# Second layer's begin: narrow products for the second group's queries and the first group's wo, fewer idle products behind w2

## The chip, the core and the metric

The kernel runs on one core of one Trainium2 chip. A core has TensorE (PE: matrix products; its loads of weights are listed as PEld), VectorE (DVE), ScalarE (ACT), GpSimd (POOL) and SyncE (SP), which here issues nearly all DMA transfers from HBM. The engines run side by side, each through its own instructions in order, and wait for one another by semaphores. SBUF holds the operands, PSUM takes the products. The metric is the device time of the core in microseconds (us); less is better.

## The reference

A decoder with two layers at one position: attention with 32 heads over a cache of 4,096 keys and values, then an MLP with a hidden width of 1,376, and the same again with the same weights and the same cache. All numbers are float32.

```
def _A_ref(x, k_cache, v_cache, wq, wo):
    q = (x @ wq) in 32 heads of 128
    scores = q . k_cache * 128 ** -0.5
    p = softmax(scores)
    o = p . v_cache
    return o @ wo                           # (1, 1, 512)

def _B_ref(x, w1, b1, w2, b2):
    h = gelu(x @ w1 + b1)                   # 1376 wide
    return h @ w2 + b2

x = A_x                                     # (1, 1, 512)
x = x + _A_ref(_layernorm(x), ...)
x = x + _B_ref(_layernorm(x), ...)
x = x + _A_ref(_layernorm(x), ...)
x = x + _B_ref(_layernorm(x), ...)
```

Keys and values are 67 MB each, and each layer needs them all; the kernel moves 285.9 MB.

## The kernel before, in words

**Groups.** The 32 heads are done in eight groups of four. A group's keys, like its values, are 8,192 KB: eight blocks of 128 partitions x 2,048 floats (`NC`), four quarters of 512 (`U`) each. A group is: queries (x by the group's 1,024 KB of wq), scores (64 PE records into `pS`), softmax weights (`exponentials`: maximum on DVE, exponential on ScalarE; `weights`: PE transposes into `pO`, which is also `pT`), values (64 records into `pO`, or for most groups three blocks on PE and five on DVE), `head` (which brings four heads' results into columns), and the product with the group's wo.

**Narrow and wide.** A product with one row of x or of the heads can be put to PE in two ways. The wide form (`wide_query_block`, L338, and the `else` of `out_product`, L281) takes a 128-column stationary operand from `x_wide` or `on_wide` and 512 moving columns: four products, eight PE records, since each is two passes; the answer is turned by four DVE transposes of 32x128 (`turned(..., wide=True)`, L148). The narrow form (`query_block`, L191, and the `if last` branch, L278) has one or two stationary columns and 128 moving ones, four products to each quarter, 32 records; its answer is turned by a single transpose of 128x128 (L150). Before, the second layer's first group has narrow queries (`first_queries`, L451), its second group wide ones (`next_queries`, L464). wo is narrow only at the end of each layer, and there it goes to `pS`.

**The arena.** Nearly all of SBUF is one tile, `arena`, with three homes for blocks of keys or values (`A_AT`, `B_AT`, `C_AT`), an area `SHARED` for w1, w2 and later a group's wq, and an area `PAIR` for a pair of weights (one group's wo and another's wq). `SCRATCH` overlaps the end of `SHARED`'s w2.

**The second layer's begin.** The first layer ends with group 7. Its keys (in `C_AT`) and values (in `A_AT`) stay, and so do group 6's values (in `B_AT`, six quarters of them parked in PSUM, `pK`, and copied back by ScalarE at L473). The second layer therefore takes group 7 first, with no load, then group 6, whose keys are loaded again into whatever comes free, then group 5 and so on. I call them the second layer's first, second and third group. The loads stand in SP's queue in this order:

1. w2's five pieces into `SHARED`, behind w1's products;
2. the second group's wq in two halves, into the place of w2's blocks 0 to 3, behind w2's blocks 1 and 3 (`behind_w2`, L435); 1,024 KB and 512 KB of its keys behind blocks 7 and 9;
3. 1,024 KB of its keys into `PAIR + NC`, behind the first group's queries (L454); then 1,024, 1,024 and 3,328 KB into `C_AT`, behind the first group's scores of block 0, 1 and 5 (L458, L460);
4. a pair of weights into `C_AT + 24 U`, behind the first group's scores (L462);
5. the third group's keys, 8,192 KB into `A_AT`, behind the first group's values (L487);
6. the third group's values: 6,144 KB into `C_AT`, behind the second group's scores, and 2,048 KB over the pair of weights, behind the third group's queries (L489, pieces (0, 6) and (6, 8));
7. the next pair, the fourth group's keys, and so on.

SP takes these one by one, and a load that has to wait holds up all behind it. PE takes its products in the order of the program (`keep_in_program_order`, L84); the order on DVE and ScalarE is the tile framework's.

**The idle products.** `idle` (L165) multiplies zeros; its result is never read. In `mlp`, where `load_w2` is given (the first layer's MLP), one of 512 columns stands behind w2's blocks 4, 7 and 9, and one of 256 behind block 10, the last.

Of the kernel before, what the change touches and what calls it, by code (L numbers as in the profile page):

```python
# [17 lines left out]
P = 128  # L18
# [7 lines left out]
FB = 11  # L26
W1C = FJ * J
EPS = 1e-5
U = 512
# [24 lines left out]
def decode_layers(ctx: ExitStack, tc: tile.TileContext, x, k, v, w, w1, b1, w2, b2, out):  # L54
# [10 lines left out]
    def small(name, n=1):  # L65
        if name not in places:
            a = sum(b - a for a, b in places.values())
            places[name] = a, a + n
        a, b = places[name]
        assert b <= 120 and b - a == n  # L70
        return smalls[:, a:b]
# [3 lines left out]
    def at(first, n):  # L75
        return arena[:, first : first + n]

    def load(first, src):
        t = at(first, src.shape[-1])
        tc.keep_in_program_order(nc.sync.dma_start(t, src))  # L80
        return t

    def matmul(*a, **kw):
        tc.keep_in_program_order(nc.tensor.matmul(*a, **kw))  # L84
# [7 lines left out]
    def of_w(row, i, n):  # L92
        return w[row][:, NC * i : NC * (i + n)]

    def by_four(t):
        return t.rearrange("p (j n) -> p j n", j=4)


    wq_t = by_four(load(SHARED, of_w(1, 0, 1)))
# [18 lines left out]
    pS, pO = (psum.tile([P, 512], F32, name=n) for n in ("pS", "pO"))  # L118
# [9 lines left out]
    def of_32(t, n, i=0):  # L128
        return t[:, : 32 * n].rearrange("p (c q) -> p c q", q=32)[:, :, i]
# [6 lines left out]
    def in_quarters(t, n):  # L136
        return t[:, : 32 * J].rearrange("p (j n) -> p j n", j=J)[:, :, :n]

    def pairs(t):
        return t[:, :8].rearrange("p (c i) -> p c i", i=2)  # L140

    def turned(src, wide=False):

        t = work.tile([P, P], F32, name="turned")
        if wide:
            for j in range(J):
                q = slice(32 * j, 32 * j + 32)
                nc.vector.transpose(t[q], src[q, P * j : P * (j + 1)])  # L148
        else:
            nc.vector.transpose(t, src[:, :P])  # L150
        return t
# [13 lines left out]
    def idle(to, n=U):  # L165
        matmul(to[:, :n], zero[:, 0:1].to_broadcast([P, P]), at(C_AT, n), start=True, stop=True)
# [22 lines left out]
    def query_block(c, xs, wt):  # L189
        for j in range(J):  # L190
            matmul(pO[32 * j : 32 * j + 2, :P], pairs(xs)[:, c, :], wt[:, c, P * j : P * (j + 1)],  # L191
                   start=(c == 0), stop=(c == 3))

    def queries(to, negm, wide=False):
        qt = turned(to, wide)
        z = zq
        nc.vector.scalar_tensor_tensor(z[:, :, C - 1], of_32(qt, J, 1), negm, of_32(qt, J),
                                       op0=ALU.mult, op1=ALU.add)
        return z
# [55 lines left out]
    def head(rl, last=False):  # L255
        ot = at(SCRATCH, U)
        nc.vector.transpose(ot, pO)  # L257
        o, on = small("o", 4), on_wide
        own = at(SCRATCH, 4 * 129).rearrange("p (b q) -> p b q", q=129)[:, :, :P]
        own = own.rearrange("p b (d q) -> p d b q", q=32)[:, :, :, 0]  # L260
        nc.vector.tensor_reduce(o, own, axis=AX.X, op=ALU.add)
        if last:
            nc.vector.tensor_scalar(on[:, :4], o, rl, None, op0=ALU.mult)
        else:
            nc.vector.tensor_scalar(in_quarters(on, 4), o.unsqueeze(1).to_broadcast([P, J, 4]), rl, None,  # L265
                                    op0=ALU.mult)
        return on

    def head_out(rl, wt, last=False):
        on = head(rl, last)  # L270
        out_product(on, wt, last)
        return of_32(turned(pS) if last else turned(pO, wide=True), 4)

    def out_product(on, wt, last=False):
        for d in range(4):
            if last:
                for j in range(J):
                    matmul(pS[32 * j : 32 * j + 1, :P], on[:, d : d + 1], wt[:, d, P * j : P * (j + 1)],  # L278
                           start=(d == 0), stop=(d == 3))
            else:  # L280
                matmul(pO, on[:, d : d + P], wt[:, d, :], start=(d == 0), stop=(d == 3))  # L281

    def mlp(xs, s, w1_t, w2_t, load_w2=None, behind_w2=None):
        xb = small("xb", 4)
        nc.gpsimd.tensor_tensor(xb, pairs(xs)[:, :, 0], b2c, op=ALU.add)
        for c in range(4):
            for j in range(J):
                matmul(pO[32 * j : 32 * j + 2, :FJ], pairs(xs)[:, c, :], w1_t[c][:, FJ * j : FJ * (j + 1)],
                       start=(c == 0), stop=(c == 3))
            if c == 0:  # L290
                nm, ss = mean_of(xs, s)
            if c == 1:
                r = rstd_of(ss)
            if load_w2:
                load_w2(c)
        idle(pS)
        ht = at(SCRATCH, 32 * FB)
        nc.vector.transpose(ht, pO[:, : 32 * FB])
        h, u, a, z, t, g = (small(f"gelu_{i}", FB) for i in "huaztg")
        nc.vector.scalar_tensor_tensor(h, of_32(ht, FB, 1), nm, of_32(ht, FB), op0=ALU.mult, op1=ALU.add)  # L300
        if load_w2:
            load_w2(4)
        nc.vector.scalar_tensor_tensor(u, h, r, b1c, op0=ALU.mult, op1=ALU.add)
        nc.vector.scalar_tensor_tensor(a, u, 0.044715, u, op0=ALU.mult, op1=ALU.mult)
        nc.vector.scalar_tensor_tensor(z, a, 1.0, u, op0=ALU.add, op1=ALU.mult)
        nc.scalar.activation(t, z, AF.Tanh, scale=float(np.sqrt(2.0 / np.pi)))
        nc.vector.scalar_tensor_tensor(g, t, 1.0, u, op0=ALU.add, op1=ALU.mult)
        for c in range(FB):
            for j in range(J):
                matmul(pS[32 * j : 32 * j + 1, :P], g[:, c : c + 1], w2_t[c][:, P * j : P * (j + 1)],  # L310
                       start=(c == 0), stop=(c == FB - 1))
            if load_w2:
                behind_w2(c)
                if c in (4, 7, 9):
                    idle(pO)
                elif c == FB - 1:
                    idle(pO, U // 2)
        return of_32(turned(pS), 4), xb

    def load_w1(first, a, b):  # L320
# [14 lines left out]
    xs, s = set_x(zero, 1.0, xcol)  # L335
# [19 lines left out]
    def next_queries(xs, negm, wt, to=pO):  # L355
        for c in range(4):
            wide_query_block(to, c, xs, wt)
        z = queries(to, negm, wide=True)
        if to is pS:
            nc.vector.memset(pS, 0.0)  # L360
        return z

    def add_up(acc, own):
        t = small("acc", 4)
        nc.vector.scalar_tensor_tensor(t, own, 1.0, acc, op0=ALU.mult, op1=ALU.add)
        return t


    def group(z, acc, ahead, k_blocks):
        if ahead:  # L370
            t, rl, wt = ahead
            sum_up(t)
            on = head(rl)
        for c, t in k_blocks:
            scores(z, c, t)
        if ahead:
            out_product(on, wt)
        p = exponentials(sc, nsc)
        if ahead:
            acc = add_up(acc, of_32(turned(pO, wide=True), 4))  # L380
        return acc, *weights(p)
# [8 lines left out]
    negm, z, sc, nsc = first_queries(xs, s, wq_t, wide=True)  # L390
    acc = pairs(xs)[:, :, 0]
    ahead = None
    for g in range(G):
        final = g == G - 1
        k_home, v_home = RING[2 * g % 3], RING[(2 * g + 1) % 3]
        acc, pt, rl = group(z, acc, ahead, blocks(k, g, k_home, HALVES if final else ((0, C),)))
# [3 lines left out]
        if g < G - 2:  # L400
# [3 lines left out]
            z = next_queries(xs, negm, by_four(pair[:, NC:]), to=pS)  # L404
# [10 lines left out]
        if final:  # L415
            wo_t = by_four(load(PAIR, of_w(g % 2, g, 1)))
# [4 lines left out]
        else:  # L421
            pair = load(PAIR, of_w(g % 2, g, 2))
            acc = add_up(acc, head_out(rl, by_four(pair[:, :NC])))
            wq_t = by_four(pair[:, NC:])
            z = next_queries(xs, negm, wq_t)
# [19 lines left out]
    xs, s = set_x(own, 0.5, xb)  # L445
# [5 lines left out]
    negm, z, sc, nsc = first_queries(xs, s, wq_t)  # L451
    acc = pairs(xs)[:, :, 0]
    wq_t = by_four(at(SHARED, NC))
# [7 lines left out]
            k_t.append(at(KEPT_K, U))  # L461
    pair = load(C_AT + 24 * U, of_w(g % 2, g - 1, 2))  # L462
    p = exponentials(sc, nsc)
    z = next_queries(xs, negm, wq_t)  # L464
    pt, rl = weights(p)
    for c in range(C):
        values(c, pt, quarters(A_AT + NC * c), c)
    acc = add_up(acc, head_out(rl, wo_t))

    v_t = [at(B_AT + U * i, U) for i in range(KEPT_V // U)]  # L470
    for i, first in enumerate([SHARED, SHARED + U] + [PAIR + U * j for j in range(4)]):
# [5 lines left out]
    pt, rl = weights(exponentials(sc, nsc))  # L477
    for c in range(C):
        values(c, pt, v_t[4 * c : 4 * c + 4], c)
    acc = add_up(acc, head_out(rl, by_four(pair[:, NC:])))  # L480
    z = next_queries(xs, negm, by_four(pair[:, :NC]))

    homes, ahead = (A_AT, C_AT, B_AT), None
    for n in range(2, G):
        g, final = G - 1 - n, n == G - 1
        k_home, v_home = homes[(2 * n - 1) % 3], homes[2 * n % 3]
        acc, pt, rl = group(z, acc, ahead, blocks(k, g, k_home, HALVES if final else ((0, C),)))  # L487
        if not final:
# [3 lines left out]
            z = next_queries(xs, negm, by_four(pair[:, :NC]), to=pS)  # L492
# [5 lines left out]
        wo_t = by_four(load(PAIR, of_w(g % 2, g, 1)))  # L498
# [52 lines left out]
```

## Time and profile before

| | us |
|---|---|
| median of three timed runs | 679.8 |
| lowest and highest of them | 678.49, 680.85 |
| the profiled execution | 677.74 |
| its span, first to last instruction | 676.0 |
| PE busy in the span | 400.3 |
| DVE busy in the span | 333.2 |
| packets of the DMA queue that SP feeds, as a share of 16 engines' span | 99.0% |

All rows of the profile and the trace come from the one profiled execution, and their times count from the start of its span. The page gives busy times, 40 equal slices of the span, the chain of work that ended last, the costliest groups and the transfers. The trace answers further views: a timeline by engine (start, busy time, line, operation, output<-input, partitions x elements, number of records, idle time before it and what ended it), transfers with the time from issue to landing, and busy time, granted clock and DMA share in chosen stretches. An idle engine costs nothing unless the chain that ends last runs through it.

### The profile page before, as it was taken

What the parts mean: (1) busy time and instruction counts of PE and PEld (TensorE: products, weight loads), DVE (VectorE), ACT (ScalarE), POOL (GpSimd) and SP (SyncE); (2) the same over time, 40 slices, a digit from 0 to 9 for tenths busy, and PEclk for the clock granted to TensorE, in tenths of its full rate; (3) what the DMA queues carried; (4) which work ended last, traced back from release to release, by engine and by line L of the source; (5) the groups of instructions that cost most, each with busy time, mean ns of one, the idle gap of its engine ahead of it and who ended that gap; (6) DMA issues with size and microseconds to landing.
All of it is one profiled execution on the core that took longest, in us unless ns stands there. A gap on an engine that the chain in (4) does not pass through costs nothing. (4 is left out here: it accounts for less than half of the span.)

```text
span 676.0 us, 5683 instructions
## 1 busy us (share of the span) xinstructions
PE 400.3 (59%) x2416; PEld 108.1 (16%) x2416; DVE 333.2 (49%) x489; ACT 22.8 (3%) x48; POOL 4.3 (1%) x21
## 2 busy tenths in 40 slices
PE   3534753637616566286777887657517456275585
PEld 1101110111101111021213222111102111021122
DVE  2049276393682945920212311295682845937622
ACT  0010000000000000001000110000000000000000
POOL 1000000000000000000000000000000000000000
PEclk9567775986769767687979998977768867687699
DMA  9999999999999999999999999999999999999997
GB/s 373 435 435 431 434 435 434 415 451 434 430 431 416 453 428 434 434 431 416 434 410 396 409 418 430 386 461 434 428 434 410 455 431 435 430 428 419 431 414 290
DMA packets 11689, 286.25 MB, mean 423 GB/s; under 512 B 1808, under 2 KB 1808, under 8 KB 3856
## 3 DMA queue, kind: packets, MB, share of 16 engines
q1 hardware_dynamic: 11232, 285.88, 99.0%
q8 instruction: 19, 0.31, 0.2%
q10 hardware_dynamic: 432, 0.01, 0.0%
q14 instruction: 6, 0.05, 0.0%
HBM read 285.88 MB, written 0.00 MB: 423 GB/s over the span
## 5 line engine op out<-in xcount | busy, mean ns | idle before, releaser
L84 PE MATMUL pS<-arena,zq 128*8 128x512 f32 x1024 | 137.4, 697 | 35.4 <-DMA arena<-in_k 31.6
L242 DVE TENSOR_TENSOR arena<-arena,turned 128x10240 f32<-128x10240 f32 x11 | 119.1, 10826 | 43.1 <-DMA arena<-in_v 43.0
L84 PE MATMUL pO<-arena,turned 128*4 128x512 f32 x584 | 94.4, 802 | 54.0 <-DMA arena<-in_v 52.4
L247 DVE TENSOR_TENSOR arena<-arena 128x2048 f32<-128x2048 f32 (+1 forms) x33 | 98.5, 2985 | 0.7
L84 PE MATMUL pO<-arena,one 128*4 128x512 f32 x88 | 20.8, 1037 | 127.1 <-DVE arena L247 127.1
L207 DVE TENSOR_REDUCE ml<-pS 128x1 f32<-128x512 f32 x16 | 11.1, 692 | 151.3 <-PE pS L84 151.3
L84 PE MATMUL pO<-arena,on_wide 128*128 128x512 f32 x112 | 51.8, 605 | 4.0 <-DVE on_wide L265 4.0
L84 PEld LDWEIGHTS pS<-arena,zq 128*8 128x8 f32 x1024 | 29.2, 99 | 150.4 <-issue 112.4
L84 PE MATMUL pS<-arena,x_wide 128*128 128x512 f32 x88 | 42.3, 624 | 4.6 <-DMA arena<-in_w 4.6
L257 DVE STREAM_TRANSPOSE arena<-pO 128x512 f32<-128x512 f32 x16 | 11.5, 717 | 58.5 <-PE pO L84 58.5
L84 PEld LDWEIGHTS pO<-arena,turned 128*4 128x4 f32 x584 | 16.3, 102 | 117.3 <-issue 114.7
L148 DVE STREAM_TRANSPOSE turned<-pO 32x128 f32<-32x128 f32 x72 | 22.3, 309 | 20.8 <-PE pO L84 20.0
L214 ACT ACTIVATE arena<-pS,mt,smalls 128x512 f32<-128x512 f32 x16 | 12.4, 777 | 493.0 <-DVE mt L212 493.0
L219 PE MATMUL pO<-ident,arena 128*128 128x128 f32 x64 | 10.6, 290 | 30.1 <-DVE turned L148 17.8
L84 PEld LDWEIGHTS pO<-arena,on_wide 128*128 128x128 f32 x112 | 20.1, 189 | 36.3 <-issue 29.5
L84 PE MATMUL pO<-arena,x_wide 128*128 128x512 f32 (+1 forms) x64 | 17.8, 468 | 9.6 <-POOL x_wide L162 6.8
L84 PEld LDWEIGHTS pO<-arena,one 128*4 128x4 f32 x88 | 1.2, 84 | 136.2 <-DVE arena L247 136.2
L84 PEld LDWEIGHTS pS<-arena,x_wide 128*128 128x128 f32 x88 | 16.5, 198 | 34.3 <-issue 17.5
L148 DVE STREAM_TRANSPOSE turned<-pS 32x128 f32<-32x128 f32 x44 | 13.7, 311 | 0.8
L219 PEld LDWEIGHTS pO<-ident,arena 128*128 128x128 f32 x64 | 7.0, 145 | 43.4 <-issue 27.4
L224 DVE STREAM_TRANSPOSE mt<-ml 128x32 f32<-128x32 f32 x16 | 3.4, 212 | 17.2 <-ACT arena L214 17.2
L84 PEld LDWEIGHTS pO<-arena,x_wide 128*128 128x128 f32 (+1 forms) x64 | 6.8, 145 | 18.3 <-POOL x_wide L162 6.8
(79 smaller groups left out, 115.5 us busy)
## 6 DMA issues: line engine op xcount, KB each, us to landing
arena<-in_w SPq DMA_DIRECT2D x13, 2048.0 KB, 11.5
arena<-in_k SPq DMA_DIRECT2D x4, 4096.0 KB, 25.2
arena<-in_v SPq DMA_DIRECT2D x2, 4096.0 KB, 39.1
arena<-in_v SPq DMA_DIRECT2D x3, 2048.0 KB, 43.3
arena<-in_v SPq DMA_DIRECT2D x1, 6144.0 KB, 26.7
arena<-in_w SPq DMA_DIRECT2D x5, 1024.0 KB, 21.4
arena<-in_w SPq DMA_DIRECT2D x6, 688.0 KB, 30.6
arena<-in_v SPq DMA_DIRECT2D x4, 1024.0 KB, 46.5
```

The lines of the kernel that those rows point to most:

```text
L84: tc.keep_in_program_order(nc.tensor.matmul(*a, **kw))
L148: nc.vector.transpose(t[q], src[q, P * j : P * (j + 1)])
L207: nc.vector.tensor_reduce(ml[:, 0:1], pS, axis=AX.X, op=ALU.max)
L214: nc.scalar.activation(p, pS, AF.Exp, bias=bias[:, 0:1], scale=sc, accum_out=ml[:, 0:1])
L219: tc.keep_in_program_order(nc.tensor.transpose(pT[:, b].rearrange("p j r -> p (j r)"), p[:, P * b : P * (b + 1)], ident))
L224: nc.vector.transpose(lt, ml)
L242: nc.vector.tensor_tensor(t, t, w.unsqueeze(2).to_broadcast([P, 4 * J * (C - BY_PE), P]), op=ALU.mult)
L247: nc.vector.tensor_tensor(a, a, b, op=ALU.add)
L257: nc.vector.transpose(ot, pO)
```

## The change

There are three edits, all at the passage from the first layer to the second.

1. The second group's queries, by `next_queries` before (wide, into `pO`), become four `query_block` calls and `queries(pO, negm)`: narrow, into `pO`, with a single transpose.
2. The first group's product with wo, by `head_out` before (wide, into `pO`), becomes narrow, into `pO`, with a single transpose. For that `out_product` takes the tile to write; other calls do what they did.
3. Behind w2's blocks in the first layer's MLP the idle product behind block 9 goes, and the one behind block 7 has 256 columns instead of 512. Those behind blocks 4 and 10 stay as they were.

No transfer is added, dropped or put elsewhere in SP's queue.

```
-        out_product(on, wt, last)
-        return of_32(turned(pS) if last else turned(pO, wide=True), 4)
-
-    def out_product(on, wt, last=False):
+        to = pS if last else pO
+        out_product(on, wt, to, last)
+        return of_32(turned(to, wide=not last), 4)
+
+    def out_product(on, wt, to, narrow=False):
         for d in range(4):
-            if last:
+            if narrow:
                 for j in range(J):
-                    matmul(pS[32 * j : 32 * j + 1, :P], on[:, d : d + 1], wt[:, d, P * j : P * (j + 1)],
+                    matmul(to[32 * j : 32 * j + 1, :P], on[:, d : d + 1], wt[:, d, P * j : P * (j + 1)],
                            start=(d == 0), stop=(d == 3))
             else:
-                matmul(pO, on[:, d : d + P], wt[:, d, :], start=(d == 0), stop=(d == 3))
+                matmul(to, on[:, d : d + P], wt[:, d, :], start=(d == 0), stop=(d == 3))
...
                 behind_w2(c)
-                if c in (4, 7, 9):
-                    idle(pO)
-                elif c == FB - 1:
-                    idle(pO, U // 2)
+                if c in (4, 7, FB - 1):
+                    idle(pO, U if c == 4 else U // 2)
...
     p = exponentials(sc, nsc)
-    z = next_queries(xs, negm, wq_t)
+    for c in range(4):
+        query_block(c, xs, wq_t)
+    z = queries(pO, negm)
     pt, rl = weights(p)
     for c in range(C):
         values(c, pt, quarters(A_AT + NC * c), c)
-    acc = add_up(acc, head_out(rl, wo_t))
+    out_product(head(rl, last=True), wo_t, pO, narrow=True)
+    acc = add_up(acc, of_32(turned(pO), 4))
```

More of the change, by code (lines that the diff above doesn't have):

```diff
@@ L376, in group @@
         if ahead:
-            out_product(on, wt)
+            out_product(on, wt, pO)
         p = exponentials(sc, nsc)
```

## The prediction

> **What bounds the kernel now.** I read the slices of the profile first, then the chain of work that ended last, then the transfers one by one around the change.
>
> ```profile
> span 676.0 us, 5683 instructions
> ...
> DMA  9999999999999999999999999999999999999997
> GB/s 373 435 435 431 434 435 434 415 451 434 430 431 416 453 428 434 434 431 416 434 410 396 409 418 430 386 461 434 428 434 410 455 431 435 430 428 419 431 414 290
> ```
>
> A slice is 676.0/40 = 16.9 us. The DMA engines are busy in every slice, and most slices move about 434 GB/s. The long dip is in the 21st to 26th slices, 338 to 439 us: 410 396 409 418 430 386. That is the change of layer, which the diff edits. Against 434 the six lack 24+38+25+16+4+48 = 155, or 155/434 x 16.9 = 6.0 us; the next slice, 461, gives 27/434 x 16.9 = 1.1 us back (a packet counts where it starts). So about 5 us is lost there, and no edit of this stretch can win more.
>
> Rows of the chain (start, us, what), behind the change:
>
> ```profile
> 474.43 31.65 DMA arena<-in_k
> 506.21 9.86 PE pS L84 x64
> ...
> 520.15 29.52 DMA arena<-in_k
> ...
> 654.04 17.85 DMA arena<-in_w
> ```
>
> Products there start when a block of keys lands (474.43 + 31.65 = 506.08, scores at 506.21), and the chain ends on the last loads of the weights. From here to the end the time is that of the bytes. What makes a product earlier is therefore worth nothing by itself; it pays only where it lets SyncE issue a transfer before the DMA engines run short.
>
> That can be read transfer by transfer. Each pair of rows is the issue (start, us it took) and the same transfer's size and us from issue to landing; the 8,192 KB blocks of keys show no size. The two rows with x2 and 6144.0 belong together: the second issue of that x2 ends at 405.18 + 23.00, so it began about 427.85.
>
> ```profile
> 368.96 0.33 SPq L80 DMA_DIRECT2D arena<-in_k  x1
> arena<-in_k SPq DMA_DIRECT2D x1, 512.0 KB, 6.9
> 372.10 0.33 SPq L80 DMA_DIRECT2D arena<-in_k  x1
> arena<-in_k SPq DMA_DIRECT2D x1, 1024.0 KB, 7.3
> 374.01 0.33 SPq L80 DMA_DIRECT2D arena<-in_k  x1
> arena<-in_k SPq DMA_DIRECT2D x1, 1024.0 KB, 7.9
> 380.02 0.33 SPq L80 DMA_DIRECT2D arena<-in_w  x1
> arena<-in_w SPq DMA_DIRECT2D x1, 2048.0 KB, 17.1
> 393.19 0.33 SPq L80 DMA_DIRECT2D arena<-in_k  x1
> arena<-in_k SPq DMA_DIRECT2D x1, 24.3
> 405.18 23.00 SPq L80 DMA_DIRECT2D arena<-in_v  x2
> arena<-in_v SPq DMA_DIRECT2D x1, 6144.0 KB, 26.7
> arena<-in_v SPq DMA_DIRECT2D x1, 2048.0 KB, 9.7
> 473.99 0.33 SPq L80 DMA_DIRECT2D arena<-in_w  x1
> arena<-in_w SPq DMA_DIRECT2D x1, 2048.0 KB, 12.7
> ```
>
> The yardstick is far from the change: the pair of weights lands at 473.99 + 12.7 = 486.7, the 8,192 KB behind it at 506.1, so 19.4 us, or 2.42 us for 1,024 KB. By that:
>
> - 1,024 KB of keys, issued 372.10, lands 379.4; the one ahead of it landed at 368.96 + 6.9 = 375.9. It took 3.5 us for 2.4: **1.1 lost**, issued 3.8 ahead of that landing.
> - The eight blocks of the third group's keys, issued 393.19, land 417.5; ahead, 380.02 + 17.1 = 397.1. 20.4 for 19.4: **1.0 lost**, issued 3.9 ahead.
> - The last 2,048 KB of that group's values, issued 427.85, land 437.5; ahead, 405.18 + 26.7 = 431.9. 5.6 for 4.8: **0.8 lost**, issued 4.0 ahead.
> - Not lost: 374.01 + 7.9 = 381.9, 2.5 us behind 379.4 for 2.4, issued 5.4 ahead; the 6,144 KB of values, 14.4 us for 14.5, issued 12.3 ahead.
>
> So a transfer issued about 4 us ahead of the landing before it loses some 1 us, and one issued 5.4 us ahead loses nothing.
>
> **The change, part by part.** PE, DVE and SP rows that price it:
>
> ```profile
> 367.23 1.12 PE L84 MATMUL pO<-arena,zero 128*128 128x512 f32 x2
> 368.28 0.62 PE L84 MATMUL pS<-arena,smalls 128*1 128x128 f32 x16
> 368.83 1.12 PE L84 MATMUL pO<-arena,zero 128*128 128x512 f32 x2
> 369.89 0.40 PE L84 MATMUL pS<-arena,smalls 128*1 128x128 f32 x8
> 370.22 0.70 PE L84 MATMUL pO<-arena,zero 128*128 128x256 f32 x2
> 370.35 0.32 DVE L150 STREAM_TRANSPOSE turned<-pS 128x128 f32<-128x128 f32 x1 [6.39 <-PE pS L84]
> 362.85 0.33 SPq L80 DMA_DIRECT2D arena<-in_w  x1
> arena<-in_w SPq DMA_DIRECT2D x1, 256.0 KB, 5.5
> ```
>
> *Idle products.* Half a one takes 0.70 instead of 1.12, so block 7's saves 0.42. Block 9's goes: block 10's products start at 369.89, 1.06 behind the idle product's start at 368.83. Block 10 would start at 369.89 - 0.42 - 1.06 = 368.41, and the transpose of the MLP's output (370.35) moves up 1.48. Late next is the last piece of w2: it lands at 362.85 + 5.5 = 368.35, 0.06 sooner. It just fits, so I take **1.4**; bounds 0.4 (the landing slips by 1) and 1.5. The last, half idle product stays, and so does its place behind block 10.
>
> ```profile
> 370.93 0.62 PE L84 MATMUL pO<-arena,x_wide 128*2 128x128 f32 x16
> ...
> 379.89 3.70 PE L84 MATMUL pO<-arena,x_wide 128*128 128x512 f32 x8
> 380.03 0.69 DVE L207 TENSOR_REDUCE ml<-pS 128x1 f32<-128x512 f32 x1 [6.44 <-PE pS L84]
> 383.63 1.29 DVE L148 STREAM_TRANSPOSE turned<-pO 32x128 f32<-32x128 f32 x4
> ...
> 386.08 7.05 PE L84 MATMUL pO<-arena,turned 128*4 128x512 f32 x64 [0.38 <-DVE turned L222]
> 394.45 3.70 PE L84 MATMUL pO<-arena,on_wide 128*128 128x512 f32 x8 [1.32 <-DVE on_wide L265]
> 405.23 0.69 DVE L207 TENSOR_REDUCE ml<-pS 128x1 f32<-128x512 f32 x1 [5.55 <-PE pS L84]
> 408.97 8.75 PE L84 MATMUL pO<-arena,turned 128*4 128x512 f32 x64 [0.42 <-DVE turned L222]
> ```
>
> *Second group's queries.* Eight wide records (3.70) become two sets of 16 narrow ones (0.62 each, 1.2), and four transposes (1.29) become one (0.32). They stand between scores and softmax weights: the weights' PE transposes write pO and must wait until the queries are read from it. Where nothing stands between, as in the second group, the maximum at 405.23 leads to the value products at 408.97, 3.74 us. Here it is 380.03 to 386.08, 6.05. So up to 2.3 are to be won. If DVE takes the one transpose and the small step behind it ahead of the exponential, about 0.4 goes back; if it takes them only behind the softmax's small steps, the gain is the shorter transposes alone, 1.29 - 0.32 = 1.0. I take **2.2**, bounds 1.0 to 2.3.
>
> *First group's wo.* 32 narrow records for 8 wide ones:
>
> ```profile
> 355.76 1.05 PE L84 MATMUL pS<-arena,on_wide 128*1 128x128 f32 x32 [0.27 <-DVE on_wide L263]
> ```
>
> 3.70 - 1.05 = **2.65** (the same form, at the first layer's end). The scores of the second group follow at once on PE; ScalarE's copies into the wo columns come free as much sooner. One transpose for four, off the path.
>
> No transfer changes its size or its place in SP's queue. Each is issued when its products end, so the 1,024 KB at 372.10 moves up 1.4, the keys of 393.19 by 1.4 + 2.2 = 3.6, the values of 405.18 and of 427.85 by 3.6 + 2.65 = 6.2. New leads: 3.8 + 1.4 = 5.2; for the keys 3.9 + 3.6 less the 1.1 by which the landing before comes earlier = 6.4; for the values 4.0 + 6.2 - 2.1 = 8.1. All three reach the leads that lost nothing, the first just so. Won: 1.1 + 1.0 + 0.8 = **2.9 us**. The other 2 us of the dip belong to pieces of w1, w2 and wq, whose issue the diff does not move. Of 6.2 us of shorter work more than half is not seen: behind 437 the products wait for landings.
>
> The profiled execution took 677.74 (span 676.0), below the 678.49 to 680.85 of the three timed runs; I take the 2.9 off both: 674.8 for a profiled one, **676.9** against the median 679.8.
>
> **The Trainium skill against it.** "DMA: Bandwidth & Descriptors" gives a first byte at about 0.6 us (Latency and other measured facts) and a fixed cost of about 2.0 us, mostly the receipt after the last byte (Anatomy of one DMA). By that, an estimate, a lead of 2.6 us would do, the three losses at 3.8 to 4.0 have another cause, and the change wins nothing. The rows above side with a longer need: 5.4 ahead lost 0.1, 4 ahead lost 1.
>
> **Rivals.** *Partly:* the first lead, 5.2, is too short or DVE's order is the bad one; then 1.0 + 0.8 = 1.8 comes: 678.0. For it: the thin 0.06 of w2. *Nothing:* the losses are the price of going from small pieces to large ones, not of a late issue: 679.8. For it: all three stand at such a step or at a lone piece; against it: 374.01 and 405.18 are steps too. *Slower:* PE's clock. The granted clock over two stretches of 5 us (after DMA columns: share, GB/s):
>
> ```profile
> 385.00:390.00 5.00, 4.55 (x44) 1.44 (x48) 0.47 (x2) 0.00 (x0) 0.00 (x0) 1.00 0.97 417
> 410.00:415.00 5.00, 5.00 (x40) 1.14 (x36) 0.00 (x0) 0.00 (x0) 0.00 (x0) 0.71 0.94 406
> ```
>
> It is 1.00 through the first group and 0.71 after the second group's softmax, where PE stood nearly still from 405.2 to 408.97; those 64 products took 8.75 instead of 7.05. The shorter products remove work that filled the first group's gap, and idle products that stood ahead. Price: scores at 9.86 (506.21) and values at 8.75 cost 2.8 + 1.7 = 4.5 in the first group, more than the 3.6 won; that is the point where it decides. The keys are then issued 0.9 late. With a third such set, the second group's scores (2.8), the last values are 1.1 late too. Lost against now 0.9 + 1.1, won 1.1 from the first piece: +0.9, 680.7; the scores at half clock throughout (14.1) would add some 4 more, 685. Against it: in the new first group PE stands still 2.76 less the 1.1 of narrow queries = 1.7 us at most. The skill's "TensorE: Matmul & The Clock Gate" (Part 1) halves the clock after an idle window of about 3.4 us; by that rule this gap costs nothing.
>
> **How the numbers follow.** Forecast 0.62, partly 0.18, nothing 0.14, slower 0.06. Low end: all 2.9 and some of the other 2 us, with the runs' spread (1.2 us to a side), 675.5. High end 679.2 keeps all of "partly" and leaves out "slower" and most of "nothing". A measurement of this kernel tells about 0.3% (2.0 us) from no change; the forecast lies 0.9 beyond that. Faster: most of the forecast's share and a third of partly's, 0.60. Same 0.35. Slower, part of its case and noise, 0.05.
>
> **What would show it.** Right: issues near 370.7, 389.6, 399.0 and 421.6; intervals between landings of 2.4, 19.4 and 4.8; value products 3.7 to 4.3 us behind the first maximum; the six slices' lack down from 6.0 to about 3. Wrong: the issues earlier but the intervals as before (nothing); a clock under 1 between 368 and 392 (slower); block 10 waiting for w2; new short slices behind 440, or a chain that no longer ends on the loads.

## The result, and the profile after

Six runs of the changed kernel had a median of 676.15 us (675.69 to 677.07), six of the kernel before 679.52 (678.49 to 680.85). The ratio is 0.995, 95% interval 0.9934 to 0.9966: 3.4 us less, by the interval 2.3 to 4.5. Forecast were 676.9, and 2.9 us less. The profiled execution took 675.69 (span 673.9), 2.05 us below that of before.

The DMA slices on the page of the changed kernel (mean busy share in tenths, GB/s):

```profile
DMA  9999999999999999999999999999999999999996
GB/s 374 436 437 436 432 433 436 414 454 436 432 436 409 459 433 436 436 433 398 428 414 389 433 446 427 437 441 433 424 428 412 452 436 433 432 428 423 432 409 276
```

The 21st to 26th slices were 410 396 409 418 430 386; now they are 414 389 433 446 427 437. The second one, with w1, w2 and wq, is as bad as it was. The third and the sixth are whole again. Against 434 the six lack 58 in all, or 2.3 us of a slice of 16.8; about 3 was foretold.

The three transfers that had come late, in the changed kernel's trace: issue, then size and us to landing, with the transfer that lands before each.

```profile
368.31 0.33 SPq L80 DMA_DIRECT2D arena<-in_k  x1
arena<-in_k SPq DMA_DIRECT2D x1, 512.0 KB, 7.1
370.29 0.33 SPq L80 DMA_DIRECT2D arena<-in_k  x1
arena<-in_k SPq DMA_DIRECT2D x1, 1024.0 KB, 7.8
...
378.20 0.33 SPq L80 DMA_DIRECT2D arena<-in_w  x1
arena<-in_w SPq DMA_DIRECT2D x1, 2048.0 KB, 18.1
390.56 0.33 SPq L80 DMA_DIRECT2D arena<-in_k  x1
arena<-in_k SPq DMA_DIRECT2D x1, 25.1
399.78 0.33 SPq L80 DMA_DIRECT2D arena<-in_v  x1
arena<-in_v SPq DMA_DIRECT2D x1, 6144.0 KB, 30.4
423.66 0.33 SPq L80 DMA_DIRECT2D arena<-in_v  x1
arena<-in_v SPq DMA_DIRECT2D x1, 2048.0 KB, 11.9
```

The 1,024 KB of keys land at 378.1, 2.7 us behind the 512 KB at 375.4 (3.5 before, 2.4 needed). The third group's keys land 19.4 us behind the pair at 396.3 (20.4 before, 19.4 needed). The last 2,048 KB of its values take 5.4 (5.6 before, 4.8 needed), but what follows them is faster: from the keys' landing to that of the fourth group's values it was 64.3 us and is 63.5.

The timeline shows what moved the issues:

```profile
368.53 0.32 DVE L150 STREAM_TRANSPOSE turned<-pS 128x128 f32<-128x128 f32 x1 [4.61 <-PE pS L84]
...
378.20 0.69 DVE L207 TENSOR_REDUCE ml<-pS 128x1 f32<-128x512 f32 x1 [6.43 <-PE pS L84]
...
379.51 0.31 DVE L150 STREAM_TRANSPOSE turned<-pO 128x128 f32<-128x128 f32 x1
...
381.94 8.54 PE L84 MATMUL pO<-arena,turned 128*4 128x512 f32 x64 [0.41 <-DVE turned L222]
...
392.69 7.05 PE L84 MATMUL pS<-arena,zq 128*8 128x512 f32 x64
...
403.99 9.46 PE L84 MATMUL pO<-arena,turned 128*4 128x512 f32 x64 [0.38 <-DVE turned L222]
```

From the first maximum (378.20) to the value products (381.94) it is now 3.74 us, where it was 6.05. But the value products take 8.54 instead of 7.05, and those of the second group 9.46 instead of 8.75. The chain still ends on the loads of the weights.

### The profile page after: what moved, and what is told of

It reads as the page before. It is cut to its first block, busy times and chain, and to the rows that moved or that the text cites. A ratio compares the mean times of both kernels' runs of the same rounds, so it can differ in the third digit from the quotient of the medians.

```text
span 673.9 us, 5767 instructions
## 1 busy us (share of the span) xinstructions
PE 398.9 (59%) x2462; PEld 107.3 (16%) x2462; DVE 331.0 (49%) x483; ACT 22.5 (3%) x48; POOL 4.3 (1%) x21
## 5 line engine op out<-in xcount | busy, mean ns | idle before, releaser
L84 PE MATMUL pS<-arena,zq 128*8 128x512 f32 x1024 | 137.4, 697 | 36.2 <-DMA arena<-in_k 31.0
L84 PE MATMUL pO<-arena,turned 128*4 128x512 f32 x584 | 98.3, 831 | 53.3 <-DMA arena<-in_v 51.7
L84 PE MATMUL pO<-arena,one 128*4 128x512 f32 x88 | 20.8, 1037 | 127.6 <-DVE arena L247 127.6
L84 PEld LDWEIGHTS pS<-arena,zq 128*8 128x8 f32 x1024 | 29.3, 100 | 150.6 <-issue 109.8
L84 PE MATMUL pO<-arena,on_wide 128*128 128x512 f32 (+1 forms) x136 | 49.2, 527 | 4.0 <-DVE on_wide L265 2.7
L84 PE MATMUL pS<-arena,x_wide 128*128 128x512 f32 x88 | 41.1, 609 | 2.7 <-DMA arena<-in_w 2.6
L84 PEld LDWEIGHTS pO<-arena,turned 128*4 128x4 f32 x584 | 16.4, 104 | 119.0 <-issue 115.2
L219 PE MATMUL pO<-ident,arena 128*128 128x128 f32 x64 | 11.1, 300 | 30.4 <-DVE turned L148 16.3
L148 DVE STREAM_TRANSPOSE turned<-pO 32x128 f32<-32x128 f32 x64 | 19.8, 309 | 18.1 <-PE pO L84 17.4
L84 PEld LDWEIGHTS pO<-arena,on_wide 128*128 128x128 f32 (+1 forms) x136 | 19.4, 164 | 34.9 <-issue 28.1
L84 PEld LDWEIGHTS pO<-arena,one 128*4 128x4 f32 x88 | 1.2, 84 | 136.7 <-DVE arena L247 136.7
L84 PE MATMUL pO<-arena,x_wide 128*2 128x128 f32 (+1 forms) x88 | 16.4, 400 | 9.6 <-POOL x_wide L162 6.7
L84 PEld LDWEIGHTS pS<-arena,x_wide 128*128 128x128 f32 x88 | 16.1, 194 | 33.1 <-DMA arena<-in_w 17.3
L219 PEld LDWEIGHTS pO<-ident,arena 128*128 128x128 f32 x64 | 7.3, 150 | 43.2 <-issue 25.1
L84 PE MATMUL pO<-arena,smalls 128*2 128x344 f32 x64 | 7.1, 536 | 4.7 <-DMA arena<-in_w 4.0
```

The source lines that it names most:

```text
L219: tc.keep_in_program_order(nc.tensor.transpose(pT[:, b].rearrange("p j r -> p (j r)"), p[:, P * b : P * (b + 1)], ident))
```

## The experiments

The lead of a transfer is the time by which it is issued ahead of the landing of the transfer before it; where it is issued after that landing, the lead is negative. Two theories. **Leads:** a shorter product counts only where it brings the issue of a transfer from under about 5 us to more than 5 us ahead of the landing before it. **Work:** the 6.2 us of shorter work gave 3.4 us, each part by its share. The first four kernels take the parts singly, the others shorten or lengthen work where the leads are already long. A single trace can be compared only where the two differ by about 1 us or more: far from the change some transfers took 0.3 to 1.8 us too long in every trace, and they were not always the same ones. The ratios and their 95% intervals are those on record; they are not the quotients of the two medians and differ from them by up to 0.0014.

**Idle products alone.**

```
     z = next_queries(xs, negm, wq_t)                  # as before
...
     acc = add_up(acc, head_out(rl, wo_t))             # as before
...
-                if c in (4, 7, 9):
-                    idle(pO)
-                elif c == FB - 1:
-                    idle(pO, U // 2)
+                if c in (4, 7, FB - 1):
+                    idle(pO, U if c == 4 else U // 2)
```

> The idle products' edit alone (block 9's gone, block 7's half); second group's queries and first group's wo wide as before. Measure: the time, and in the trace the stretch from the landing of the first layer's last values to the landing of the fourth group's values (before 481.82 - 351.85 = 129.97 us, after 479.14 - 351.82 = 127.32). Theory of leads (a transfer issued under about 5 us ahead of the landing before it loses what is missing to 5; shorter products count only there): the lead of the 1,024 KB of keys behind the first queries rises from 3.8 to 5.2, 1.1 us won; the other two leads stay near 4 (3.9 + 1.4 - 1.1 = 4.2, and 4.1), 0.3 won. Stretch 128.6, time 678.1. Theory of work (the 6.2 us of shorter PE work gave 3.4 us, each part by its share, 0.54): 1.4 x 0.54 = 0.8, stretch 129.2, time 678.7.

677.48 against 678.67, ratio 0.999 (0.998 to 0.9999); the stretch 129.5. The first keys were issued at 370.27, lead 5.15, as expected. Then this, from the timeline and the transfers of this kernel:

```profile
378.19 0.33 SPq L80 DMA_DIRECT2D arena<-in_w  x1
arena<-in_w SPq DMA_DIRECT2D x1, 2048.0 KB, 17.6
393.06 0.33 SPq L80 DMA_DIRECT2D arena<-in_k  x1
arena<-in_k SPq DMA_DIRECT2D x1, 24.1
...
384.25 8.75 PE L84 MATMUL pO<-arena,turned 128*4 128x512 f32 x64 [0.38 <-DVE turned L222]
```

The first group's values ran at a lower clock, 8.75 us for 7.05, which took back 1.7 of the 1.8 us: the third group's keys were issued at 393.06, as before. The pair landed at 395.8, though, sooner than before, so their lead was 2.8, and they landed at 417.2: 21.4 us for 19.4. What the first lead won the second lost. Neither theory had that; the loss itself is the leads'.

**Queries alone, wo alone, both without the idle products' edit.**

```
+    for c in range(4):                                # queries alone, and both
+        query_block(c, xs, wq_t)
+    z = queries(pO, negm)
...
+    out_product(head(rl, last=True), wo_t, pO, narrow=True)    # wo alone, and both
+    acc = add_up(acc, of_32(turned(pO), 4))
```

> The second group's narrow queries alone. Theory of leads: the first loss (1.1) stays; the third group's keys are issued 2.2 sooner, lead 6.1, 1.0 won; its last values' lead becomes 4.0 + 2.2 - 1.0 = 5.2, 0.8 won. Together 1.8: stretch 128.2, time 677.7. Theory of work: 2.2 x 0.54 = 1.2, stretch 128.8, time 678.3.

> The first group's narrow wo alone. Theory of leads: it comes behind the issue of the third group's keys, so only the last values' lead rises, 4.0 + 2.65 = 6.7: 0.8 won at most, stretch 129.2, time 678.7. Theory of work: 2.65 x 0.54 = 1.4, stretch 128.6, time 678.1.

> Narrow queries and narrow wo, the idle products as before. Theory of leads: as the queries alone, for their 5.2 is enough for the last values: 1.8 won, stretch 128.2, time 677.7; the changed kernel is better by the first loss alone, about 1. Theory of work: (2.2 + 2.65) x 0.54 = 2.6, stretch 127.4, time 676.9, 1.4 better than the queries alone.

| kernel | us (before 678.67) | ratio | stretch (before 130.0) | third keys: lead, needed 19.4, took | last values: lead, needed 4.8, took |
|---|---|---|---|---|---|
| queries | 677.36 | 0.9984 (0.9973 to 0.9995) | 127.9 | 6.4, 19.3 | 5.9, 4.9 |
| wo | 678.16 | 1.000 (0.9989 to 1.0011) | 128.4 | 4.2, 20.0 | 7.0, 4.9 |
| both | 677.35 | 0.9985 (0.9974 to 0.9996) | 127.9 | 6.3, 19.3 | 9.9, 4.9 |

The times side with the leads: both together are what the queries are alone, 677.35 and 677.36, though PE's path is 2.65 us shorter, and with the idle products' edit the change reaches 0.995 (0.9966 when timed again, below). wo alone lengthened one lead and left the keys' at 4.2; its time did not move by what a measurement shows, and its stretch was nearer to what work foretold (128.6) than leads (129.2). For the two transfers in the table each row is what the theory of leads says: where the lead is over 5 the transfer takes what it needs.

**The same on: second group's wo and third group's queries narrow too.**

```
-    acc = add_up(acc, head_out(rl, by_four(pair[:, NC:])))
-    z = next_queries(xs, negm, by_four(pair[:, :NC]))
+    out_product(head(rl, last=True), by_four(pair[:, NC:]), pO, narrow=True)
+    acc = add_up(acc, of_32(turned(pO), 4))
+    for c in range(4):
+        query_block(c, xs, by_four(pair[:, :NC]))
+    z = queries(pO, negm)
```

> The changed kernel, and also the second group's wo and the third group's queries narrow, as the first group's wo and the second group's queries already are. That shortens PE's path by another 2.65 + 2.3 = about 5 us ahead of the issue of the third group's last values (423.66 in the changed kernel). Theory of leads: that lead is 430.15 - 423.66 = 6.5 us already and becomes about 11; nothing is won: stretch 127.3, time as the changed kernel, 676.2. Theory of work: another 5 x 0.54 = 2.7 us, stretch 124.6, time 673.5.

```profile
398.61 0.33 SPq L80 DMA_DIRECT2D arena<-in_v  x1
arena<-in_v SPq DMA_DIRECT2D x1, 6144.0 KB, 31.9
414.76 0.33 SPq L80 DMA_DIRECT2D arena<-in_v  x1
arena<-in_v SPq DMA_DIRECT2D x1, 2048.0 KB, 20.7
```

The last values were issued 8.9 us sooner than in the changed kernel, 15.7 ahead of the landing before them (430.5), and landed at 435.5, to 0.1 us as in the changed kernel (423.66 + 11.9). 676.63, ratio 0.9968 (0.9956 to 0.998); stretch 126.9. Work had asked for 673.5 and 124.6. It falls.

**Three idle products ahead of the third group's queries, and behind them.** Each multiplied zeros with a quarter of `A_AT`:

```
     acc = add_up(acc, head_out(rl, by_four(pair[:, NC:])))
+    for i in range(3):                                # ahead
+        idle(pS, home=A_AT)
     z = next_queries(xs, negm, by_four(pair[:, :NC]))
+    for i in range(3):                                # behind, in the other kernel
+        idle(pS, home=A_AT)
```

> The changed kernel with three idle products of 512 columns (about 1.06 us each, 3.2 together) ahead of the third group's queries, so ahead of the issue of its last values. Theory of leads: the lead falls from 6.5 to 3.3, 1.7 short of 5: stretch 129.0, time 677.9. Every us of PE counts: 3.2 more, stretch 130.5, time 679.4. PE's work is hidden altogether: no change.

> The same three idle products directly behind the third group's queries, ahead of its scores: the issue of the last values is not touched, and the next issue that the scores hold, the fourth group's values (432.4), lies 27 us ahead of the landing before it (459.8). Theory of leads: nothing lost, stretch 127.3, time 676.2; the two kernels differ by 1.7 us through the place alone. Every us of PE counts: as with the three ahead.

702.73 (ratio 1.0355, 1.0334 to 1.0377) and 710.67 (1.0459, 1.0434 to 1.0485): no theory had anything like it. `A_AT` is where the third group's keys go, and their load stands behind these products in the program, so it waited for them (41.0 us in the kernel with three ahead), and all of SP's queue behind it. The two kernels do not test what they were made for, but they are the longest delays of a load in this study. First the one ahead, then the one behind:

```profile
378.84 0.33 SPq L80 DMA_DIRECT2D arena<-in_w  x1
arena<-in_w SPq DMA_DIRECT2D x1, 2048.0 KB, 17.5
420.23 0.33 SPq L80 DMA_DIRECT2D arena<-in_k  x1
arena<-in_k SPq DMA_DIRECT2D x1, 22.4
```

```profile
379.16 0.33 SPq L80 DMA_DIRECT2D arena<-in_w  x1
arena<-in_w SPq DMA_DIRECT2D x1, 2048.0 KB, 18.2
427.35 0.33 SPq L80 DMA_DIRECT2D arena<-in_k  x1
arena<-in_k SPq DMA_DIRECT2D x1, 22.6
```

The keys were issued 23.9 and 30.0 us behind the landing of the pair and landed 46.3 and 52.6 behind it, so 26.9 and 33.2 were lost. Against the changed kernel's 676.15, timed beside another set of runs, the two are slower by 26.6 and 34.5. Loss and time go nearly one for one. All kernels' third group's keys in one row, by lead:

| lead | -30.0 | -23.9 | 2.8 (idle alone) | 4.0 (before) | 4.2 (wo) | 5.3 to 7.0 (nine kernels) |
|---|---|---|---|---|---|---|
| lost of 19.4 | 33.2 | 26.9 | 2.0 | 1.0 | 0.7 | at most 0.15 |

**One idle product in the gap of the first group's softmax.**

```
     z = queries(pO, negm)
+    idle(pO, home=A_AT)
     pt, rl = weights(p)
```

> The changed kernel with one idle product of 512 columns behind the second group's queries, where PE waits for the first group's exponential anyway. In the changed kernel the granted clock was 0.5 from 381.6 to 385.0, and the first group's value products took 8.6 us in place of 7.05. If too little PE work in the stretch before made the clock fall, it stays at 1.00 there, the values take 7.05 and the third group's keys are issued about 1.5 us sooner (near 389.1). Theory of leads: their lead was 396.27 - 390.56 = 5.7 already, so nothing is won: stretch 127.3, time 676.2. If the clock's fall cost time: up to 1.5 less, 674.7.

676.21, ratio 0.9961 (0.9946 to 0.9976). Stretches of 3 us (busy times by engine, granted clock, DMA share, GB/s) of the changed kernel, and then of this one with its value products:

```profile
381.00:384.00 3.00, 2.58 (x16) 0.69 (x20) 0.86 (x6) 0.00 (x0) 0.00 (x0) 0.60 1.04 442
```

```profile
381.00:384.00 3.00, 2.58 (x22) 0.83 (x24) 1.01 (x6) 0.49 (x2) 0.00 (x0) 1.00 1.14 485
...
382.62 7.05 PE L84 MATMUL pO<-arena,turned 128*4 128x512 f32 x64 [0.42 <-DVE turned L222]
```

The clock stayed, the keys were issued at 389.73 with a lead of 6.6 for 5.7, and the time is the changed kernel's: the fall of the clock had cost nothing. Whether the idle product kept it up is open, for it stayed up without one in three other kernels with the same first group.

**Once more: three ahead, three behind, beside the changed kernel.** The same edits, with `home=KEPT_K`, a quarter that nothing overwrites later.

> The three idle products ahead of the third group's queries once more, now reading a quarter of the arena that no later load writes (KEPT_K), so that they hold up nothing but PE. Measure beside the time: from the landing of the third group's keys to that of the fourth group's values, 26,624 KB, 62.9 us at 2.42 us for 1,024 KB (before 481.82 - 417.50 = 64.3, changed 479.14 - 415.62 = 63.5, both groups narrow 63.3). Theory of leads: the last values' lead falls from 6.5 to about 3.3; by the runs so far a lead of 2.75 lost 2.0 and one of 4.0 lost 1, so 1.5 lost: 64.6, and 1.2 to 1.5 us slower than the changed kernel beside it. Every us of PE counts: 3.2 slower. PE's work is hidden altogether: no difference.

> The same three directly behind the third group's queries. The issue of the last values stays near 423.7 with its lead of 6.5; the fourth group's values, issued 3.2 later, are still 24 us ahead. Theory of leads: 63.2 us in that stretch, time as the changed kernel beside it. Every us of PE counts: 3.2 slower, as with the three ahead.

> The changed kernel as it is, to stand beside the other three on the same chip: about 0.995 of before.

Ahead 676.91 (0.9972, 0.9959 to 0.9986), behind 675.98 (0.9952, 0.9937 to 0.9966), the changed kernel 676.78 (0.9966, 0.9951 to 0.998), before 678.32. Three products at either place cost nothing that shows. But the lead that I had meant to shorten was not shortened. The kernel with three ahead:

```profile
398.38 0.33 SPq L80 DMA_DIRECT2D arena<-in_v  x1
arena<-in_v SPq DMA_DIRECT2D x1, 6144.0 KB, 31.8
421.82 0.33 SPq L80 DMA_DIRECT2D arena<-in_v  x1
arena<-in_v SPq DMA_DIRECT2D x1, 2048.0 KB, 13.1
...
415.62 2.74 PE L84 MATMUL pS<-arena,zero 128*128 128x512 f32 x6
```

The idle products ran while DVE turned wo's answer, which the queries wait for anyway. From the start of wo to that of the queries it was 6.11 us (412.08 to 418.19) for 5.18 in the changed kernel, so only 0.9 of the 2.74 stood on PE's path; with the three behind it is the same, 6.18 from the queries to the scores for 5.31. And in this execution the clock held through the first group's values (issue of the first values at 398.38 for 399.78). So the last values were issued 8.4 us ahead, not 3.3. The two runs speak against the 3.2 us that I had foretold for work, but 0.9 of PE's path is about what an interval leaves open, so they decide little between the theories. A lead of 3 at this place was not tried.

**No idle product behind w2.**

```
             if load_w2:
                 behind_w2(c)
-                if c in (4, 7, FB - 1):
-                    idle(pO, U if c == 4 else U // 2)
```

> The changed kernel with no idle product at all behind w2's blocks. w2's last pieces then hold up PE (they landed at 366.03, 367.32 and 367.95 in the changed kernel; block 10 started near 368.1), so at most 0.3 us comes ahead of the transpose of the MLP's output. Theory of leads: the first keys' lead is 5.1 already; nothing won, time as the changed kernel. If the idle products behind w2 keep the clock up for the first group (rival of the prediction): the granted clock falls below 1 between 371 and 390, the 64 scores or the 64 values take 8.6 us or more in place of 7.05, and the third group's keys' lead (5.7) falls to 4.1 or less: 0.5 to 1 us slower.

676.31, ratio 0.9968 (0.9954 to 0.9982): the changed kernel's time. The first group's scores took 7.05 and its values 8.51, as in the changed kernel (7.05, 8.54). Since the clock had fallen there already, this run doesn't show what the full set of idle products did: the four kernels that have it (before, queries, wo, both) all took 7.05 for the first group's values, and of the ten with fewer six took 8.5 and more. A count in the next section bears on that.

## Why the prediction was right, and where it was not

**The three losses.** It took 1.1 + 1.0 + 0.8 = 2.9 for transfers issued some 4 us ahead, and 2.9 was forecast; the two timings of the change gave 3.4 (2.3 to 4.5) and, in the second, 0.0034 of 678.32, 2.3 (1.4 to 3.3). Keys: 1.0 foretold, 1.0 won. First keys: issued at 370.29 for 370.7; 3.5 us became 2.7, 0.8 of 1.1. But the pieces behind them took longer, and over 14 traces it varies: the 6,400 KB from these keys on, 15.1 by the yardstick, took 16.1 to 17.0 in the five with a lead under 4.5, 15.4 to 16.1 in the nine with 4.8 or more (before 16.5, changed 15.95).

Last values: 0.8 in the stretch behind the keys (64.3 to 63.5), but that the sum agrees with 0.8 is luck. The piece that I had named won 0.3 (5.7 to 5.4), and the 6,144 KB ahead of it took 0.2 more. The other 0.7 came from the fourth group's keys and values, 8,192 KB each and issued more than 13 us ahead both times, which took 19.6 and 19.8 before and 19.4 now. In the other traces the piece does as foretold: 5.8 us where it was issued 4.0 ahead (idle alone), 4.7 to 4.9 in the eleven where it was 5.9 or more.

That leads are the cause is shown best by what won nothing (wo on top of the queries, 5 us of narrower products further on) and by the row of leads above. "Nothing", the rival in which the step from small to large pieces costs by itself, falls with it: the same step took at most 19.5 whenever it was issued 5.3 us ahead or more.

What the prediction overlooked stands in the very trace that it read. w2's first piece, also of before:

```profile
358.27 0.33 SPq L80 DMA_DIRECT2D arena<-in_w  x1
arena<-in_w SPq DMA_DIRECT2D x1, 512.0 KB, 4.1
```

The load ahead of it lands at 361.06, so its lead was 2.8, yet it took 1.3 us for 1.2. In all 14 traces its lead was 2.8 to 4.1 and its loss at most 0.07. The first half of wq, also 512 KB, was issued 3.2 to 3.9 ahead in 13 traces and lost 0.4 to 1.5. So "4 us ahead loses some 1 us" holds for the three transfers from which it was read and not for every one. Whether the size decides, or whether a loss shows only at a later landing, was not tested.

**The rule of the Trainium skill** that was weighed ("DMA: Bandwidth & Descriptors", Latency and other measured facts; Anatomy of one DMA) would, by my estimate, have made a lead of 2.6 us enough. The section on the anatomy is on transfers that GpSimd issues, and these are SP's. The third group's keys with a lead of 2.8 lost 2.0; w2's first piece with the same lead lost nothing that shows.

**Idle products.** 1.4 was taken; the transpose came 1.82 sooner (370.35 to 368.53), for w2's last piece landed at 367.95 instead of 368.33 and did not hold up block 10.

**Queries.** 2.2 taken, 2.3 measured (6.05 to 3.74). DVE put the one transpose (379.51) between the small steps ahead of the exponential, and it delayed nothing that shows.

**wo.** 2.65 taken; from the end of the values (the issue of the keys) to the second group's scores it was 4.89 (393.19 to 398.08) and is 2.13 (390.56 to 392.69): 2.8.

**What failed: the clock.** The prediction set the fall of PE's clock in the first group aside, since PE would stand still 1.7 us there and the Trainium skill's "TensorE: Matmul & The Clock Gate" (Part 1) asks for an idle window of about 3.4. It stood still 1.86 us, and the clock fell, in the changed kernel and in four more of the eight with that first group: 8.5 us and more for 7.05. The rule as I used it does not hold here. That is why the keys were issued at 390.56 and not at 389.6, and the last values, with 9.46 for 8.75 in the second group, at 423.66 and not at 421.6. The price of one such fall, 1.5 us, fits into leads of 5.7 and 6.5, so it cost no time; the point that the prediction named, 3.7 us and more, was not reached. With the idle products' edit alone it did cost: there the lead fell to 2.8.

The traces show more of it. In each of them the changes of the granted clock lie whole multiples of 3.41 us apart (in the changed kernel at 381.6, 385.0, 402.1 and 408.9), and each trace has this grid of steps elsewhere. Two steps of the changed kernel, then the same two of the one with three ahead (busy time of PE's L84 products alone, granted clock, DMA share, GB/s):

```profile
378.20:381.60 3.40, 0.81 (x32) 1.00 1.09 460
381.60:385.00 3.40, 3.06 (x16) 0.50 1.00 426
```

```profile
378.00:381.40 3.40, 1.10 (x36) 1.00 1.12 470
381.40:384.80 3.40, 2.75 (x28) 1.00 0.99 421
```

The emptiest step around the first group's softmax held 0.57 to 0.91 us of these products in the six traces in which the clock then fell, and 1.10 to 1.71 in the seven without a product put into the gap in which it stayed; with the PE transposes (L219) counted in, the two sets would meet near 1.55. So by this count the clock falls behind the same gap or not by where the gap lies in the grid, and that was luck. The idle products behind w2 end before 372, and that step begins at 377.9 or later, so they are not in it. This was counted afterwards, and no run tests it. It gives no threshold either: a step of 1.71 (358.9 us, three behind on `A_AT`) and one of 1.29 (429.2 us, three ahead on `KEPT_K`), far from this gap, were followed by half clock too.

## What to carry to other kernels

Where the DMA queue is full nearly all the time, list for each transfer how long before the previous landing it is issued and how long it then takes beyond its bytes. Only transfers that lose time by this list are worth work, and the products ahead of their issue are what to shorten. Past the lead that suffices nothing more is won, but the room is worth having: it pays for a fall of the clock. A test product that reads a buffer is also a reader that the buffer's next load waits for.

## What the runs showed that I had not expected

The third group's keys need nearly 5 us of lead, not 2 or 3, before they lose nothing: 2.8 lost 2.0, 4.0 lost 1.0, 4.2 lost 0.7, 5.3 none. That is no rule for every transfer: w2's first piece did with 2.8, and three of the later pairs of weights, issued 6.3 to 7.2 ahead, lost 1.2 to 1.8 where the other pairs lost 0.1 at most. With negative leads the loss is the delay and 3.0 to 3.2 us more. Why the loss sets in nearly 2 us sooner than that is open; that the 16 engines run out at different times would do it, and was not tested.

The granted clock can fall when PE does not stand still for long: in the changed kernel between narrow products, PE transposes and gaps of at most 1.86 us. With the same first group it stayed up in three traces of eight. By the count above it is the place of the gap in a grid of 3.41 us that decides; a run that tests it is missing.
